# Linear attention with a maxout MLP on one core: the first k heads issued by ScalarE instead of SyncE

## The chip, the cores and the metric

The kernel runs on one core of one Trainium2 chip. The metric is device time in microseconds. The median of three runs before the change was 319.77 us (319.64 to 320.38).

## The reference

Inputs are q, k and v of shape (8 batches, 8 heads, 1024 positions, 64), two projections E and F of shape (64, 1024), and three MLP weights. All are float32.

```python
k_proj = np.einsum('ks,bhsd->bhkd', E, k)        # 1024 positions -> 64 rows
v_proj = np.einsum('ks,bhsd->bhkd', F, v)
attn   = softmax(q @ k_proj.T / sqrt(64))        # over the 64 rows
x      = (attn @ v_proj), heads side by side     # (8192, 512)
out    = np.maximum(x @ w1, x @ w2) @ w_out      # (8192, 512)
```

## The kernel before

TensorE does all the products in half precision. The batches of attention are worked one after the other, and the MLP of one batch is interleaved with the attention of the next through a list of slots that is written out by hand. Only the start of the program, batch 0, matters for the change.

The sequence on each engine is the order in which the program is written (a manual schedule). At the start:

- SyncE (queue q1 in the profile) issues three plain loads in float32: E into `ef_sb[:, 0]`, the first two heads of batch 0's k into `kf_sb`, and F into `ef_sb[:, 1]` (lines 86 to 88). `kf_sb` is "uncast": it arrives as float32 and is cast to half precision on the core.
- ScalarE loads its function table (line 89).
- GpSimd (queue q0) issues all the loads that cast to half precision on the way (line 108): heads 2 and 3 of k, heads 0 to 3 of q, heads 4 to 7 of k, heads 4 to 7 of q, then v in four pairs of heads. The MLP weights follow (lines 130, 139 and 143), each held back until earlier loads have landed.
- TensorE begins with eight filler matmuls on a tile of ones, `warm(8)` (line 153). Further `warm` calls stand between the steps of batch 0.

Then come the steps of batch 0 (lines 958 to 991), in this order on TensorE:

1. `step_eft(0)` transposes E (line 167); VectorE copies it out as `eft` (line 173).
2. The two heads in `kf_sb` are cast into `k_sb`: head 0 by VectorE (line 959), head 1 by ScalarE (line 960).
3. `step_kv(t, 0, 4, "k")` projects heads 0 to 3 of k (line 195). It needs `eft`, both casts, and GpSimd's heads 2 and 3.
4. `step_eft(1)` transposes F, `step_kpt` transposes the projected k (line 285), `step_qt` transposes q (line 311).
5. `step_sc` computes scores (line 340) and their exponentials on ScalarE (line 380); `step_dn` sums them (line 352) and takes the logarithm (line 388).
6. The same for heads 4 to 7, and then the projections of v (line 195 again), two heads at a time as v lands, followed by `step_at`, which applies the weights to v, and the first MLP products (line 524).

Of the kernel before, what the change touches and what calls it, by code (L numbers as in the profile page):

```python
# [19 lines left out]
def kernel(  # L20
# [12 lines left out]
    nc = tc.nc  # L33
# [5 lines left out]
    NC = S // 128  # L39
# [25 lines left out]
    def mm_bank(dtype=FP32, n=None):  # L65
        if n is None:
            n = turn.pop(0)
            turn.append(n)
        return ps.tile([128, 512 if dtype == FP32 else 1024], dtype, tag=f"mm{n}", name="mm_ps")
# [9 lines left out]
    def big(n, dtype=FP16):  # L79
# [3 lines left out]
    kf_sb = const.tile([128, 2048], FP32, tag="wo", name="kf_sb")[:, 0 : 2 * NC * D].rearrange(  # L83
        "p (h c d) -> p h c d", h=2, d=D
    )
    nc.sync.dma_start(out=ef_sb[:, 0, :], in_=E)
    nc.sync.dma_start(out=kf_sb, in_=k[0, 0:2].rearrange("h (p c) d -> p h c d", c=NC))
    nc.sync.dma_start(out=ef_sb[:, 1, :], in_=F)
    nc.scalar.add_instruction(
        mybir.InstLoadActFuncSet(  # L90
# [4 lines left out]
            outs=[],  # L95
        )
    )


    def alloc(t, n):  # L100
# [27 lines left out]
    for g in range(2):  # L128
        for w_sb, w in ((w2_sb, moe_w2), (w1_sb, moe_w1)):
            nc.gpsimd.dma_start(  # L130
                out=w_sb.rearrange("p (g z) f -> p g z f", z=2)[:, g, :, 0:256],
                in_=w.rearrange("(g p z) f -> p g z f", p=128, z=2)[:, g, :, 0:256],
            )
    for w_sb, w, f0, f1 in (
# [3 lines left out]
        for z in range(2):  # L138
            nc.gpsimd.dma_start(
                out=w_sb.rearrange("p (g z) f -> p g z f", z=2)[:, :, z, f0:f1],  # L140
                in_=w.rearrange("(g p z) f -> p g z f", p=128, z=2)[:, :, z, f0:f1],
# [994 lines left out]
    for i, (new, old) in enumerate(zip([*groups[1:], none], groups)):  # L1136
        n, h = divmod(i + 2, 2)
# [54 lines left out]
    for reg in regs:  # L1192
# [4 lines left out]
        out=mm_bank()[0:1, 0:1], lhsT=ones16[:, 0:1], rhs=ones16[:, 0:1], start=True, stop=True  # L1197
# [166 lines left out]
```

## Time and profile before

| | |
|---|---|
| median of 3 runs | 319.77 us |
| profiled execution, device time | 319.9 us |
| its span, first to last instruction | 318.1 us |
| TensorE busy | 312.3 us (98%) |
| VectorE, ScalarE, GpSimd busy | 241.1, 206.2, 40.8 us |
| GpSimd's DMA queue q0 | 30688 packets, 28.05 MB |
| SyncE's DMA queue q1 | 45664 packets, 24.85 MB |
| ScalarE's DMA queue q10 | 288 packets, 0.20 MB, all at the end of the run |

The profile is of one execution. Times in it count from the start of the program. A line of the timeline has the start, the duration, the engine, the line of the kernel, what is written and read, and in brackets the idle time of the engine just before and what ended it. SPq and ACTq are the DMA issues of SyncE and ScalarE. The profile does not give the landing time of loads issued by SyncE; it is read from the instruction that waited for them.

### The profile page before, as it was taken

To read this page: it belongs to the slowest core of one execution; us is meant where nothing else is said; L and a number is where in the kernel's file an instruction comes from. 1 tells how busy PE (TensorE), PEld (TensorE's weight loads), DVE (VectorE), ACT (ScalarE), POOL (GpSimd) and SP (SyncE) were. 2 spreads that over 40 slices of the span, in tenths; PEclk is the share of its full clock that TensorE was granted. 3 is DMA by queue.
4 is the path that set the end of the run, shared out by engine and by line. 5 is a ranking of instruction groups with operands and counts; after the bars stand their busy time and mean duration, and the time that the engine had idled before them with its cause. 6 is when DMAs were issued, how large, how long until landed. Compare 5 with 4: busy or idle time off the path is not lost.

```text
span 318.1 us, 9308 instructions
## 1 busy us (share of the span) xinstructions
PE 312.3 (98%) x3922; PEld 253.6 (80%) x3922; DVE 241.1 (76%) x441; ACT 206.2 (65%) x373; POOL 40.8 (13%) x63
## 2 busy tenths in 40 slices
PE   8989999999999999999999999999999999999996
PEld 3555588888887888788887888788887888888885
DVE  2366888877969696996969696996969696969883
ACT  2476842777776777477776778477776777765541
POOL 8259002003000300022000400030000000000000
PEclk9999999999999999999999999999999999999999
DMA  7999999999979999899999999989979131313124
GB/s 189 206 200 195 207 206 202 207 158 160 204 139 195 162 212 245 210 182 154 223 233 217 167 204 245 215 151 183 232 149 209 45 102 36 102 35 102 36 99 136
DMA packets 76684, 53.71 MB, mean 169 GB/s; under 512 B 29664, under 2 KB 76128, under 8 KB 76640
## 3 DMA queue, kind: packets, MB, share of 16 engines
q0 software_dynamic: 30688, 28.05, 56.0%
q1 hardware_dynamic: 45664, 24.85, 32.7%
q8 instruction: 31, 0.51, 0.6%
q10 hardware_dynamic: 288, 0.20, 0.2%
q14 instruction: 13, 0.11, 0.1%
HBM read 57.15 MB, written 16.78 MB: 232 GB/s over the span
## 4 chain that ended last, share of the span: by engine, by line
PE 92%; DMA 5%; POOL 1%; ACT 1%; issue 0%; DVE 0%; POOLq 0%
PE mm_ps L837 47%; PE mm_ps L745 27%; PE mm_ps L524 4%; DMA v_sb<-in_v_dram 4%; PE att_ps L352 3%; PE mm_ps L195 3%; PE mm_ps L340 2%; PE mm_ps L633 2%; PE att_ps L237 1%; DMA out_dram<-o_sb 1%; PE mm_ps L311 1%; POOL k_sb L108 0%; POOL q_sb L108 0%; ACT ld_sb L388 0%; ACT ex_sb L380 0%
## 5 line engine op out<-in xcount | busy, mean ns | idle before, releaser
L719 ACT COPY p_sb<-mm_ps 128x512 f32<-128x512 f32 x179 | 101.8, 592 | 49.1 <-PE mm_ps L745 27.2
L837 PEld LDWEIGHTS <-big 128*128 128x128 f16 x768 | 73.5, 98 | 11.8 <-issue 3.6
L837 PE MATMUL mm_ps<-T_sb,big 128*128 128x256 f16 x576 | 76.9, 273 | 0.0
L760 DVE TENSOR_TENSOR gt_sb<-mm_ps,p_sb 128x512 f16<-128x512 f32 x56 | 38.5, 687 | 43.0 <-PE mm_ps L745 41.6
L745 PE MATMUL mm_ps<-big,big 128*128 128x256 f16 x336 | 50.4, 273 | 0.0
L745 PEld LDWEIGHTS <-big 128*128 128x128 f16 x448 | 43.8, 98 | 5.1
L837 PE MATMUL mm_ps<-wo_sb,gt_sb 128*128 128x256 f16 x256 | 42.6, 273 | 0.0
L837 PEld LDWEIGHTS <-gt_sb 128*128 128x128 f16 x376 | 35.7, 98 | 6.7 <-issue 2.7
L469 ACT ACTIVATE ex_sb<-mm_ps 128x512 f16<-128x512 f32 x50 | 27.2, 596 | 18.0 <-PE mm_ps L340 12.3
L745 PEld LDWEIGHTS <-wd_sb 128*128 128x128 f16 x336 | 32.9, 98 | 3.8
L745 PE MATMUL mm_ps<-xt_sb,wd_sb 128*128 128x256 f16 x224 | 32.8, 273 | 0.0
L499 DVE TENSOR_TENSOR xt_sb<-att_ps,ld_sb 128x1024 f16<-128x1024 f32 x26 | 31.7, 1219 | 0.2
L837 PE MATMUL mm_ps<-m_sb,xt_sb 128*128 128x256 f16 x128 | 24.4, 273 | 0.0
L303 POOL COPY junk<-qt_sb 1x1 f16<-1x1 f16 x6 | 2.1, 346 | 172.5 <-DMA qt_sb<-q_sb 172.5
L868 DVE TENSOR_TENSOR o_sb<-mm_ps,p_sb 128x512 f32<-128x512 f32 x32 | 21.9, 683 | 2.8 <-ACT p_sb L897 2.0
L763 DVE TENSOR_SCALAR gt_sb<-gt_sb 128x512 f16<-128x512 f16 (+1 forms) x60 | 20.9, 348 | 2.1
L705 DVE TENSOR_TENSOR big<-gt_sb 128x1024 f16<-128x1024 f16 x32 | 21.8, 683 | 0.0
L837 PE MATMUL mm_ps<-wo_sb,big 128*128 128x256 f16 x128 | 21.5, 273 | 0.0
L806 ACT ACTIVATE gt_sb<-mm_ps 128x512 f16<-128x512 f32 x28 | 16.8, 601 | 5.7 <-PE mm_ps L745 5.7
L837 PE MATMUL mm_ps<-T_sb,gt_sb 128*128 128x256 f16 x120 | 20.3, 273 | 0.0
L837 PEld LDWEIGHTS <-xt_sb 128*128 128x128 f16 x188 | 18.3, 98 | 2.3 <-issue 0.2
L760 DVE TENSOR_TENSOR gt_sb<-p_sb 128x512 f16<-128x512 f32 x28 | 19.1, 682 | 0.6 <-ACT p_sb L719 0.6
(121 smaller groups left out, 434.7 us busy)
## 6 DMA issues: line engine op xcount, KB each, us to landing
out_dram<-o_sb SPq DMA_DIRECT2D x62, 256.0 KB
k_sb<-in_k_dram POOLq DMA_DIRECT2D x7, 1024.0 KB, 9.8
v_sb<-in_v_dram POOLq DMA_DIRECT2D x7, 1024.0 KB, 15.3
q_sb<-in_q_dram POOLq DMA_DIRECT2D x5, 1024.0 KB, 23.0
q_sb<-in_q_dram POOLq DMA_DIRECT2D x6, 512.0 KB, 15.8
big<-in_moe_w_dram POOLq DMA_DIRECT2D x12, 128.0 KB, 6.3
v_sb<-in_v_dram POOLq DMA_DIRECT2D x4, 256.0 KB, 13.6
wo_sb<-in_moe_w_out_dram POOLq DMA_DIRECT2D x1, 1024.0 KB, 10.4
```

The source lines that it names most:

```text
L195: nc.tensor.matmul(out=kv_ps[r * KP : (r + 1) * KP, h * D : (h + nh) * D], lhsT=eft[i][:, c, :], rhs=t[w][:, h0 + h : h0 + h + nh, c, :], ...
L469: nc.scalar.activation(out=t["ex", g, j][:, e, :], in_=banks[e], func=ACTF.Exp, scale=scale)
L499: nc.vector.tensor_tensor(out=x_out(t, g, j).rearrange("q z o n -> q o z n"), in0=at_ps.rearrange("q o (z n) -> q o z n", z=2), in1=ld[:, ...
L524: nc.tensor.matmul(out=h_ps, lhsT=wd_sb[:, r, fb * 128 : (fb + 1) * 128], rhs=t["xt"][:, r, :, j * W : (j + 1) * W], start=(r == 0), stop= ...
L705: nc.vector.tensor_tensor(out=S(i), in0=S(0) if x is None else x, in1=y(), op=op)
L719: copy(out=x, in_=bank)
L745: nc.tensor.matmul(out=bank[:, m * W : (m + 1) * W], lhsT=w_[:, n_, (2 * d + m) * 128 : (2 * d + m + 1) * 128], rhs=a[:, n_, :], start=(n ...
L760: nc.vector.tensor_tensor(out=c_blk(j, c), in0=two(x), in1=two(y), op=ALU.add)
L763: nc.vector.tensor_scalar_max(ap, ap, 0.0)
L806: nc.scalar.activation(out=out, in_=in_, func=ACTF.Relu)
L837: nc.tensor.matmul(out=bank[i][:, 0:CH] if two_banks else bank[:, i * CH : (i + 1) * CH], lhsT=a(c)[:, i * 128 : (i + 1) * 128], rhs=w_(c) ...
L868: nc.vector.tensor_tensor(out=o_sb, in0=two(x), in1=two(y), op=ALU.add)
```

## The change

SyncE no longer issues the load of `kf_sb`. ScalarE issues it, in its own DMA queue, as the instruction behind the table load. SyncE's queue holds E and then F. No other instruction is added, removed or moved.

```diff
     nc.sync.dma_start(out=ef_sb[:, 0, :], in_=E)
-    nc.sync.dma_start(out=kf_sb, in_=k[0, 0:2].rearrange("h (p c) d -> p h c d", c=NC))
     nc.sync.dma_start(out=ef_sb[:, 1, :], in_=F)
     nc.scalar.add_instruction(
         mybir.InstLoadActFuncSet(
...
     )
+    nc.scalar.dma_start(out=kf_sb, in_=k[0, 0:2].rearrange("h (p c) d -> p h c d", c=NC))
```

## The prediction

> **What bounds the kernel now.** I read the page first, then the chain of waits over the first 40 us, then the timeline of the first 20 us, then the DMA queues window by window. The page's chain says who sets the end:
>
> ```profile
> PE 92%; DMA 5%; POOL 1%; ACT 1%; issue 0%; DVE 0%; POOLq 0%
> ```
>
> TensorE carries 92% of it. The edited transfers matter only where TensorE is not yet the bound, in the start; a shift there moves everything behind it. The start of the chain, in order of time (start, us, what):
>
> ```profile
> 5.54 13.33 DMA v_sb<-in_v_dram
> 18.88 0.04 issue
> 18.92 0.64 PE mm_ps L195 x16
> ```
>
> So the start ends on a transfer of GpSimd's queue: the second quarter of v lands at 18.88, and its projection starts at 18.92. Before that the edited transfers count only if they delay TensorE past it. The timeline (start, duration, engine, line, in brackets the idle time before and its releaser):
>
> ```profile
> 1.26 0.83 POOL L108 DMA_DIRECT2D k_sb<-in_k_dram  x1 [0.80 <-POOLq L1348]
> 1.43 0.57 SPq L87 DMA_DIRECT2D kf_sb<-in_k_dram  x1
> ...
> 2.04 0.50 SPq L88 DMA_DIRECT2D big<-in_F_dram  x1
> ...
> 6.55 0.62 ACT L960 CAST k_sb<-kf_sb 128x512 f16<-128x512 f32 x1 [4.51 <-DMA kf_sb<-in_k_dram]
> 6.73 0.51 DVE L959 CAST k_sb<-kf_sb 128x512 f16<-128x512 f32 x1
> 7.29 0.79 PEld L195 LDWEIGHTS <-eft 128*64 128x64 f16 x8 [0.52 <-DVE k_sb L959]
> ```
>
> ScalarE waited 4.51 us for kf_sb, up to 6.55. Its cast ends at 7.17, VectorE's at 7.24, and the k projection starts at 7.29: a later landing of kf_sb delays TensorE at once, after a slack of about 0.07 us. Now what TensorE waits for near the end of the start:
>
> ```profile
> 17.34 0.41 PE L340 MATMUL att_ps<-qt_sb,kpt_sb 64*32 64x256 f16 x16
> 18.03 0.64 PE L195 MATMUL mm_ps<-v_sb,eft 128*64 128x128 f16 x16 [0.28 <-DMA v_sb<-in_v_dram]
> 18.92 0.64 PE L195 MATMUL mm_ps<-v_sb,eft 128*64 128x128 f16 x16 [0.25 <-DMA v_sb<-in_v_dram]
> ```
>
> Two waits for v, 0.28 + 0.25 = 0.53 us together, are the cushion that a delay from 7.29 meets before it reaches the end. The steps between offer none that I count: q lands just as the weight load at 10.35 wants it, and the rest runs back to back with the filler matmuls of L153, which stay the same in number.
>
> The queues (q1 is SyncE's, q0 GpSimd's; packets, MB, share of 16 engines), first from 3.25 to 4, then from 6.25 to 6.75, then from 7.25 to 8.25:
>
> ```profile
> q1 hardware_dynamic: 95, 0.19, 99.8%
> ```
> ```profile
> q1 hardware_dynamic: 46, 0.18, 96.5%
> q0 software_dynamic: 14, 0.01, 11.4%
> ```
> ```profile
> q0 software_dynamic: 194, 0.20, 123.1%
> ```
>
> kf_sb alone, in packets of 2 KB, goes at some 120 packets per us (90 without the 4-byte ones, in 0.75 us). GpSimd's packets (1 KB written, 2 KB read) reach 194 per us alone. F's 4 KB packets run from 6.06 to 7.0, behind the last of kf_sb; in that time GpSimd's queue nearly stands still.
>
> **The change, part by part.** The bytes stay the same: E and F 256 KB each, kf_sb 512 KB. In units of one 2 KB read these are 128, 128 and 256; GpSimd's first k transfer is 256 more.
>
> SyncE loses one issue of 0.57 us and gives F at 1.43 in place of 2.04. Nothing waits for SyncE then; its next issue is at 16.76. Worth nothing by itself.
>
> ScalarE gains one issue. No row has an issue behind a table load; two ACTq issues at the end of the run took 1.25 us, so 0.63 each. The table load runs from 0.75 to 2.03, so the issue is at 2.03 to 2.66. It lies in the 4.51 us in which ScalarE waits for this very transfer: cost nothing as an instruction; without that cover 0.63 us. Nothing is queued behind it on ScalarE but the cast that needs it.
>
> From issue to first packet: E was issued at 0.76 and its first packet ran at 2.16, so 1.40; the last ACTq store was issued at 314.20 and had no packet by 315.20, so over 1.0. kf_sb's first packet then comes at 3.0 to 3.4 (I take 3.4, the row that also opens a queue at the start). In the trace of before it came at 3.1, behind E. So the later issue costs only 0.3 us. What costs more is F, which now goes right behind E, ahead of or beside kf_sb.
>
> How late does kf_sb land? At 3.25 some 250 of its units are left, F's 128, and GpSimd's 256, which start at 4.1: 634. Up to 4.0 the engines carry 120 per us (one queue, the row above) or at most 200 (two at once, the 194): 90 to 150. From 4 to 5 the trace of before has 174 packets, the ceiling again 200. That leaves 284 to 370 at 5.0, and at 200 per us all three are through at 6.4 to 6.85. Before, kf_sb's last data ran at 6.05 and its cast began at 6.55. If kf_sb is the last of the three, the casts start 0.35 to 0.8 later, at 6.9 to 7.35; I take 7.15, a shift of 0.6. Less the slack of 0.07, TensorE's k projection starts 0.53 late, between 0.3 and 0.75.
>
> GpSimd's first k heads are needed by the same projection and share the same 6.4 to 6.85, so they bind no later than kf_sb with its cast of 0.62 us behind it.
>
> F is needed at 8.28, right behind the projection, and landed only just before, since its last data ran at 7.0. It now lands by about 6: worth at most 0.1 us, which I leave out.
>
> GpSimd's later transfers (q, k, q, v) decide the end. Either its stop around 6.5 was F's doing, and then it gains up to 0.43 us (97 packets in half a microsecond at 194, less the 14 that it moved), or its second transfer was not ready before 6.75, and it gains nothing. Its first 256 packets were just about used up by 6.25 (215 by 6.0, 45 in the quarter behind it), so I take the second: no gain, v at 18.88 as before.
>
> The sum: 0.53 late at the k projection, less 0.53 of waiting for v, is 0.0; with the ends 0.3 and 0.75 it is 0 to +0.2. For the parts of the cushion that I may overcount I add 0.1. The profiled execution took 319.9 us (318.1 of span, 1.8 around it), 0.13 above the median of 319.77. Forecast: 319.9 + 0.1 = **320.0 us**, practically no change.
>
> One rule of the Trainium skill speaks for little: DMA: Bandwidth & Descriptors, "Issuing engines are not separate DMA queues", says that transfers given by different engines run on the same 16 engines and interleave, so that spreading them saves only issue time. By it alone F's units would displace kf_sb's one for one, which is the lower rate in the sum above, and the sum would be +0.2. In this trace the single q1 ran below the later ceiling, which leaves room for two queues.
>
> **The rivals.**
>
> *Slower: kf_sb meets GpSimd's queue at full speed.* If ScalarE's issue waits for more than the table load's 1.28 us, kf_sb starts after 4.1 and shares packet for packet with q0. For a start at 4.6: 256 units at half of 200 per us are 2.6 us, so 7.2, and with the straggling of 0.75 that the last engine showed (29 units were left at 5.0, enough for 0.3 us, and it took until 6.05) 7.2 to 7.95; 0.5 more to the cast: 7.7 to 8.45. TensorE is 1.1 to 1.8 late, less the cushion 0.53: +0.6 to +1.3, about 321.1. It passes 0.3% when the cast starts after 8.1. The same price comes without a late issue if the slowest engine alone hands kf_sb on late: from 4.1 to 6.05 it moved some 8 packets, 0.25 us each, and six more would be 1.5 us. For it: the next ScalarE instruction in the trace is at 6.55, so nothing shows that it is free at 2.03. Against it: the rows show no activity of ScalarE after 2.03. The Trainium skill, ScalarE: Activation LUTs, "What ACT_TABLE_LOAD costs", adds a drain of about 1.38 us behind a load of 1.28; the load agrees with 1.28 here, the drain is not seen in any run, and with it the estimate is an issue at 3.4 and the upper part of this rival. A colder TensorE clock does not come into it: between 21 and 23 us TensorE is busy 0.72 and 0.53 of the time and the granted clock stays 1.00.
>
> *Faster: the queues run side by side.* If ScalarE gives the transfer while the table still loads (0.8), kf_sb runs beside E from 2.2, all three are through by about 5, and q0 has the engines to itself. q0 gains up to the 0.43 of the unused rate between 3.25 and 5 (634 - 284 against 634 - 370 units, 86 in all) and the 0.43 of the stop; TensorE loses nothing at 7.29, where the first cast holds it. The end comes earlier by 0.5 (the cushion, behind which TensorE itself is the bound) to 0.9: 319.0 to 319.4. Against it: q0's start at 4.1 and its second transfer may not depend on q1 at all.
>
> *It does not do what it says:* kf_sb was limited by its own 256 descriptors, not by its place, and lands as before: 319.9.
>
> **How the numbers follow.** About 0.3% (1 us) is what a measurement of this kernel can tell from no change. Forecast (0 to +0.4) 0.42; slower rival 0.34; faster rival 0.20, of which 0.11 past the bound, since it takes both its gains; no shift 0.04. Within 0.3%: 0.42 + 0.04 + 0.09 = 0.55; faster 0.11; slower 0.34. The range goes from 319.2 (-0.7, into the faster rival) to 321.3 (+1.4, the slower one's upper end).
>
> **What would show it.** An ACTq issue near 2.0 to 2.7 and F's 4 KB packets ahead of 4.5; ScalarE's first cast near 7.15 instead of 6.55; the k projection near 7.8; the waits of 0.28 and 0.25 for v mostly gone; the second v projection still at 18.9 to 19.1. A cast after 8.1 shows the slower rival, v landing before 18.5 the faster one. The forecast is wrong if the shift of the second v projection and that of the total differ by more than 0.3 us: then something behind the start moved.

## The result, and the profile after

The changed kernel takes 321.73 us in the median of 7 runs (320.11 to 323.0), against 320.04 (319.64 to 320.38) in now seven runs of the kernel before: 1.7 us longer, a ratio of 1.0051 with a 95% interval of 1.0037 to 1.0066. The prediction was 320.0 us, "practically no change", with 321.3 as its upper end; the result lies above that. The profiled execution took 322.0 us (span 320.2, before 318.1).

The page's chain now has no transfer of v, and less DMA:

```profile
PE 95%; DMA 2%; ACT 1%; DVE 1%; issue 0%
```

The chain of waits says what took the place of v in the start (start, us, what):

```profile
0.76 5.56 DMA big<-in_E_dram
6.32 0.14 issue
6.45 1.07 PE mm_ps L167 x8
7.52 1.79 PE mm_ps L153 x5
9.30 1.85 PE mm_ps L195 x8
```

The start hangs on E, which SyncE still issues first. The timeline of the changed kernel shows when everything is issued and used:

```profile
0.75 1.28 ACT L88 ACT_TABLE_LOAD   x1 [0.75 <-PEq L1348]
0.76 0.61 SPq L86 DMA_DIRECT2D big<-in_E_dram  x1
0.78 0.45 ACTq L97 DMA_DIRECT2D kf_sb<-in_k_dram  x1
...
1.42 0.57 SPq L87 DMA_DIRECT2D big<-in_F_dram  x1
...
5.02 0.62 ACT L960 CAST k_sb<-kf_sb 128x512 f16<-128x512 f32 x1 [2.98 <-DMA kf_sb<-in_k_dram]
...
6.45 1.07 PE L167 MATMUL mm_ps<-ident,big 64*128 64x64 f32 x8 [1.58 <-DMA big<-in_E_dram]
...
9.23 1.92 PE L195 MATMUL mm_ps<-k_sb,eft 128*64 128x256 f16 x8
```

Before the change, E's transposes and the k projection were these:

```profile
4.99 1.09 PE L167 MATMUL mm_ps<-ident,big 64*128 64x64 f32 x8
...
7.29 1.06 PE L195 MATMUL mm_ps<-k_sb,eft 128*64 128x256 f16 x8
```

ScalarE's issue does not stand behind the table load: it runs at 0.78, while the table loads. The k heads are cast from 5.02, which is 1.5 us earlier than before. But TensorE stands still for 1.58 us waiting for E, whose transposes begin at 6.45 in place of 4.99. And the k projection, 1.06 us long before, now takes 1.92.

The queues from 2 to 3.25 us and from 3.25 to 3.5 (q10 is ScalarE's, q1 SyncE's; packets, MB, share of the 16 DMA engines):

```profile
q10 hardware_dynamic: 183, 0.37, 88.5%
```
```profile
q10 hardware_dynamic: 48, 0.09, 91.7%
q1 hardware_dynamic: 5, 0.02, 24.0%
```

In the first of these windows q1 has no packet at all. E begins at 3.35, when the k heads are nearly through; before, it began at 2.16.

The trace records TensorE's granted clock in stretches of 3.41 us. The two that matter in the changed kernel (from:to, length, then the busy time and in brackets the instructions of TensorE, of its weight loads, of VectorE, ScalarE and GpSimd; then the granted clock, the DMA share and GB/s):

```profile
4.55:7.96 3.41, 1.83 (x13) 1.24 (x12) 0.41 (x1) 0.62 (x1) 3.15 (x5) 1.00 1.18 190
7.96:11.37 3.41, 3.41 (x15) 1.72 (x13) 0.80 (x3) 0.00 (x0) 0.70 (x1) 0.50 1.24 203
```

In the 3.41 us that contain the wait TensorE is busy for 1.83, and for the next 3.41 us its clock is halved. That is the 1.92 us of the k projection.

The steps of the profiled executions, as lateness in us against before. The last column is the first stretch of half clock after the clock had been full once, or the moment from which it was first full:

| | E transposes (4.99) | k projection (7.29) | F transposes (8.30) | first MLP product (23.32) | span (318.1) | TensorE clock |
|---|---|---|---|---|---|---|
| changed kernel | +1.46 | +1.94 | +2.78 | +2.05 | +2.1 | half 7.96 to 11.37 |
| the same, run again | +0.99 | +1.45 | +1.41 | +0.67 | +0.7 | full from 4.66 |

The two rows are the same kernel. Up to the k projection they differ by 0.5, and E's transposes already by as much. What holds the k projection itself is not the same: in the first row the five filler matmuls ahead of it run into the half clock (1.79 us in the chain above, 1.25 before) and end last; in the second it waits for heads 2 and 3, which GpSimd's queue brings:

```profile
8.74 1.03 PE L195 MATMUL mm_ps<-k_sb,eft 128*64 128x256 f16 x8 [0.52 <-DMA k_sb<-in_k_dram]
```

By the trace's completion records these heads landed at 7.12 before, and at 8.80 and 8.61 in the two rows: the new order made them late too, not only E. Between the k projection and the F transposes the first row then loses 0.84 to the half clock (the projection alone takes 1.92 - 1.06 = 0.86 longer). What reaches the end is the rest behind a cushion of 0.73 to 0.74.

### The profile page after: what moved, and what is told of

Read it like the earlier page. It is cut to its first block, busy times and chain, and to the rows that moved or that the text cites. A ratio compares the mean times of both kernels' runs of the same rounds, so it can differ in the third digit from the quotient of the medians.

```text
span 320.2 us, 9308 instructions
## 1 busy us (share of the span) xinstructions
PE 313.0 (98%) x3922; PEld 254.5 (79%) x3922; DVE 241.0 (75%) x441; ACT 206.2 (64%) x373; POOL 40.7 (13%) x63
## 4 chain that ended last, share of the span: by engine, by line
PE 95%; DMA 2%; ACT 1%; DVE 1%; issue 0%
PE mm_ps L837 46%; PE mm_ps L745 27%; PE mm_ps L524 4%; PE mm_ps L195 4%; PE att_ps L352 4%; PE mm_ps L340 2%; PE mm_ps L633 2%; DMA big<-in_E_dram 2%; PE mm_ps L153 1%; PE att_ps L237 1%; PE mm_ps L311 1%; PE mm_ps L167 1%; DMA out_dram<-o_sb 1%; ACT ex_sb L380 1%; PE att_ps L340 0%; DVE qt_sb L316 0%
```

## The experiments

After the result there were four theories. A: the k heads' packets go ahead of E's, E is late, and the idle TensorE loses its clock besides. B: two queues at once slow E, in whatever order. C: the clock costs nothing, since v holds the end anyway. D: E is slow for a reason other than GpSimd's queue beside it.

**The order alone, and the queue alone.** `e1_act_behind_e` leaves the k heads on ScalarE's queue, but behind E:

```diff
+    ones16 = const.tile([128, 512], FP16)
+    nc.vector.memset(ones16, 1.0)
+    nc.scalar.copy(out=flag, in_=ones16[0:1, 0:1])
     nc.scalar.dma_start(out=kf_sb, ...)
...
-    ones16 = const.tile([128, 512], FP16)
-    nc.vector.memset(ones16, 1.0)
```

> ScalarE still issues the two k heads in its own queue, but a one-element copy that waits for VectorE's tile of ones (ready at 1.41) stands before the issue, so that it comes at about 1.5, after E's issue (0.76 to 1.37). Theory A (the issue ran at 0.78 beside the table load, and the k heads' packets went ahead of E's): E is first again, its transposes start at 5.0 as before the change, the TensorE clock stays at 1.00, and the total is within 0.5 us of before (about 320). Rival B (two queues at once are what slows E, in whatever order): the E transposes stay late, 6 or more, and the total stays 1.5 to 2 us above before.

`e2_sp_kf_first` puts all three on SyncE's queue again, the k heads first:

```diff
+    nc.sync.dma_start(out=kf_sb, ...)
     nc.sync.dma_start(out=ef_sb[:, 0, :], in_=E)
-    nc.sync.dma_start(out=kf_sb, ...)
     nc.sync.dma_start(out=ef_sb[:, 1, :], in_=F)
```

> Everything on SyncE's queue as before the change, but in the order k heads, E, F. Theory A (what costs is E behind the k heads): E transposes near 6.4, a stretch of half clock, and a total 1.5 to 2 us above before, as with the change. Rival B (the second queue is the cause): E comes 512 KB later on one queue but without the contention, transposes before 5.8, clock 1.00, total within 0.6 us of before.

The first has 320.07 us, a ratio of 1.0005 (0.9996 to 1.0015) to before; the second 321.58, 1.0055 (1.0025 to 1.0085). Their timelines, e1 first:

```profile
0.76 0.61 SPq L86 DMA_DIRECT2D big<-in_E_dram  x1
...
1.42 0.57 SPq L87 DMA_DIRECT2D big<-in_F_dram  x1
1.45 0.45 ACTq L100 DMA_DIRECT2D kf_sb<-in_k_dram  x1
...
5.00 1.09 PE L168 MATMUL mm_ps<-ident,big 64*128 64x64 f32 x8
...
7.83 1.03 PE L196 MATMUL mm_ps<-k_sb,eft 128*64 128x256 f16 x8 [0.56 <-DMA k_sb<-in_k_dram]
```
```profile
0.75 0.46 SPq L86 DMA_DIRECT2D kf_sb<-in_k_dram  x1
...
1.27 0.59 SPq L87 DMA_DIRECT2D big<-in_E_dram  x1
...
7.65 1.06 PE L167 MATMUL mm_ps<-ident,big 64*128 64x64 f32 x8 [2.59 <-DMA big<-in_E_dram]
```

On ScalarE's queue with E ahead there is no loss; on one queue with E behind the k heads there is the whole loss (in the profiled execution, 323.1 us, E transposes +2.66, span +3.2, clock half from 9.08 to 12.50). Order is what costs, not the second queue: B falls. But e2 is not the changed kernel's loss in every part: E's transposes were expected near 6.4 and came at 7.65, since E took 3.92 us from its first packet to its last completion, against 2.36 before. Why is open, and the ten times of e2 reach from 319.83 to 323.9. In e1 the k projection is still 0.54 late, since it waits for GpSimd's heads; the first MLP product is 0.09 late.

`e10_ahead_of_table` is the changed kernel with ScalarE's issue written ahead of the table load (the two statements change places).

> The changed kernel with ScalarE's issue written ahead of the table load. If the table load never held the issue (it ran at 0.78 beside the load), the k heads' first packets are again near 1.9 to 2.0, E's at 3.35, and all is as with the change. If the load held it at all, the issue comes earlier by that.

The issue ran at 0.75 in place of 0.78, the k heads' first packets came in the same quarter of a microsecond, E's at 3.43; one time, 321.83 us. The table load held the issue by 0.03 us at most.

**One after the other, by the end of the issue.** `e5_act_e` gives E to ScalarE and leaves SyncE the k heads and F; `e6_act_behind_f` holds ScalarE's issue of the k heads until GpSimd's identity is there:

```diff
-    nc.scalar.dma_start(out=kf_sb, ...)
...
                 make_identity(nc, ident)
+                nc.scalar.copy(out=flag, in_=ident[0:1, 0:1])
+                nc.scalar.dma_start(out=kf_sb, ...)
```

> ScalarE issues E behind its table load; SyncE's queue carries the k heads and then F. Theory A in the form that the first runs left (one transfer after the other across both queues, in the order in which the issues end): whichever of the two issues ends first goes first. If that is E, its packets start near 1.9, its transposes at 5.0 (the fillers end there), clock 1.00, total within 0.4 us of before; if the k heads end first, E is late and the total is 1.5 us or more above. Rival B (two queues are served at once): E and the k heads have packets in the same quarters of a microsecond from 2 on, and both land late.

> The k heads on ScalarE's own queue, but issued only when GpSimd's identity is there (about 2.75), after both of SyncE's issues have ended (1.99). Theory A (one after the other, by the end of the issue, whichever the queue): the first packet of the k heads comes only when F's packets are through, near 5, as with all three on SyncE's queue in the order E, F, k heads (there 5.25), and the casts are near 8. Rival B (the two queues are served at once): the k heads have packets from about 3.9, beside F's, and the casts are near 7.

The timelines of e5, with E's transposes, and of e6, with a cast:

```profile
0.76 0.47 SPq L86 DMA_DIRECT2D kf_sb<-in_k_dram  x1
0.79 0.57 ACTq L97 DMA_DIRECT2D big<-in_E_dram  x1
...
6.48 1.07 PE L167 MATMUL mm_ps<-ident,big 64*128 64x64 f32 x8 [1.42 <-DMA big<-in_E_dram]
```
```profile
1.41 0.57 SPq L87 DMA_DIRECT2D big<-in_F_dram  x1
...
2.72 0.43 ACTq L122 DMA_DIRECT2D kf_sb<-in_k_dram  x1
...
9.99 0.62 ACT L961 CAST k_sb<-kf_sb 128x512 f16<-128x512 f32 x1 [7.09 <-DMA kf_sb<-in_k_dram]
```

In e5 the issue of the k heads ends at 1.23 and E's, on ScalarE, at 1.36; the k heads go first and E is late (transposes at 6.48, 321.63 us, ratio 1.0056, 1.0040 to 1.0073). In e6 the k heads have a queue of their own and are issued at 2.72, yet their first packet comes at 5.66, when F's are nearly through; casts at 9.99, one time of 324.85 us. That is the order that A expected, though later than its 5 and 8. All orders seen fit the same rule: in the changed kernel k (1.23) before E (1.37), in e1 k (1.90) before F (1.99), in e5 k before E. By the start of the issue it would be E first in the changed kernel (0.76 against 0.78) and F first in e1 (1.42 against 1.45). A preference for ScalarE's queue is excluded by e5. But in both pairs where start and end disagree it is the load of the k heads that ends first and goes first, so no run tells the end of the issue from some other advantage of that load, and no trace shows why it goes first.

**The order that the prediction had summed.** `e4_sp_kf_last` has E, F and then the k heads, all on SyncE's queue.

> SyncE's queue in the order E, F, k heads: the part of the change that the prediction priced, without ScalarE. By the prediction's sum the casts of the k heads start near 7.15 instead of 6.55, the k projection starts about 0.5 late, the clock stays at 1.00, and the total is 0 to 0.4 us above before. If the prediction's sum itself was wrong (the k heads meet GpSimd's queue and land after 8), the total is 0.6 to 1.3 us above before.

It took 321.76 us, 1.0062 (1.0032 to 1.0091).

```profile
8.34 0.62 ACT L960 CAST k_sb<-kf_sb 128x512 f16<-128x512 f32 x1 [6.31 <-DMA kf_sb<-in_k_dram]
```

Not 7.15 but 8.34: the k heads' packets began only at 5.31, behind the last of F. So the second alternative is right on the casts; the total, 1.7 us above before, is more than either has. The profiled execution (320.75 us) had the k projection 1.72 late and the first MLP product 0.94. The ten times split by the clock: the five with a mean granted clock of 0.995 or less take 322.1 to 324.2, the five above 320.1 to 321.4. In e2 they do not split so: its three slowest, 323.4 to 323.9, have a mean of 1.0.

**GpSimd's queue beside E.** `e7_gpsimd_held` lets GpSimd make its identity first and begin its loads only when E is there (`nc.gpsimd.tensor_copy(out=flag, in_=ef_sb[0:1, 0, 0:1])` ahead of them).

> The changed kernel, with all of GpSimd's loads held back until E has landed (a diagnosis, not a version to use: these loads come about 4 us later, so the total rises by 3 to 4 us). E's packets start at 3.35 behind the k heads as in the changed kernel. Theory A with GpSimd's queue as the reason that E then took 2.9 us for 64 packets in place of 1.1: E's packets are through by 4.6 and its transposes start by 5.6. Rival D (E is slow behind the k heads for another reason): transposes still at 6.2 or later.

E's transposes began at 6.03, between the two forecasts. With GpSimd's loads beside E, other executions of the changed start have 5.90 (e9), 5.96 (e10), 5.98 (run again) and 6.45, so holding GpSimd's queue back shows no gain. The trace's records of packets and completions say the same. From E's first packet to its last completion it took 2.36 us before (2.16 to 4.52) and 2.54 in e7; with the changed start it took 2.38 to 2.47 in e3, e8, e9, e10 and the second profile of the changed kernel, and 2.96 in its first. So in most executions E's transfer is hardly slower behind the k heads; it begins 1.2 to 1.4 us later. What stretched it in the first profile, in e5 (2.76) and in e2 is open. The time, 323.01 us, holds the later loads.

**The clock.** Three runs tried to keep TensorE busy while it waits for E: 15 fillers in place of 8 (`e3_more_fillers`), eight longer ones (`e8_long_fillers`), and the five fillers behind the transposes moved in front (`e9_fillers_moved`, 13 and 0 in place of 8 and 5).

> The changed kernel with 15 filler matmuls in place of 8 ahead of the E transposes, so that TensorE stays busy until about 6.4 while it waits for E. Theory A with the clock as a part of its cost: the transposes stay at about 6.45, the granted clock stays at 1.00, the k projection and what follows lose the 0.9 us of the half clock, total about 0.8 to 1.0 us below the changed kernel. Rival C (the clock costs nothing, since the v landings hold the end anyway): total as the changed kernel, within 0.3 us.

> The changed kernel with the same number of instructions, its eight fillers made longer (the tile of ones read as float32, 256 columns) so that TensorE is busy until about 6.4. The run with 15 fillers kept the clock and gained 0.5 us up to the last matmul, but its end came 2.7 us later behind that matmul, which I put down to its added instructions. Theory A with the clock as a part: clock 1.00 throughout, first MLP products 0.5 to 0.9 us earlier than in the changed kernel, total 0.5 to 0.9 us below it, no longer end. Rival C (the clock is worth nothing): total within 0.3 us of the changed kernel.

> The changed kernel with the five fillers behind the E transposes moved in front of them (13 and 0 in place of 8 and 5), so that the number of instructions stays and TensorE is busy until about 5.95 while it waits for E. Theory A with the clock as a part: transposes still at 6.4, clock 1.00 in the first 20 us, the k projection takes 1.1 in place of 1.9 us, first MLP products 0.5 to 0.9 us earlier than in the changed kernel and the total as much lower, near 321.0; the end behind the last matmul as before. Rival C (the clock is worth nothing): total within 0.3 us of the changed kernel run beside it.

`e3` took 323.85 us (1.0110, 1.0073 to 1.0147), `e8` 324.44 (1.0141, 1.0115 to 1.0167), `e9` 323.05 (1.0087, 1.0065 to 1.0109). All miss the total that was expected, for two reasons.

In e3 the clock stayed at 1.00 from 4.22 on, and the first MLP product came 1.20 late in place of 2.05: a gain of 0.85, in the range expected for the clock. At the k projection it was still as late as the changed kernel (1.98 against 1.94), so the gain lies behind it, where the half clock had been. But its last matmul, at 317.68, is followed by 4.6 us before the end of the span, where before it is 1.9. e8 has the same tail; its fillers were also too long (the transposes began at 7.81), so it tells nothing on the clock. Both programs have more instructions (9322 and 9324 in place of 9308; e8 was meant to have the same number), and none of those with 9308 to 9310 has the tail. Its cause was not tested.

In e9 the move only shifted the idle time behind the transposes, where TensorE waits for GpSimd's heads and had no fillers left:

```profile
4.18:7.59 3.41, 2.65 (x16) 1.45 (x13) 0.58 (x1) 0.62 (x1) 3.41 (x5) 1.00 0.97 184
7.59:11.00 3.41, 2.15 (x24) 1.91 (x24) 0.86 (x3) 0.05 (x1) 0.80 (x2) 1.00 1.18 189
11.00:14.42 3.42, 3.42 (x28) 2.34 (x25) 1.09 (x3) 0.53 (x1) 0.85 (x2) 0.50 1.24 203
```

The clock holds behind the stretch with 2.65 us of work and is halved behind the one with 2.15. The profiled k projection was 1.56 late, yet the first MLP product 2.11: here the clock cost more than the cushion gave back. All ten executions show 0.995 or less.

**The changed kernel once more**, beside e9:

> The changed kernel itself, beside the run with moved fillers. Theory A: E's transposes 1 to 2 us late again and a median 1.2 to 2 us above before; the single times spread over 2 to 3 us, where before spreads over 1, because the stretch of half clock comes in some executions and not in others.

321.25 us (320.56 to 323.79), ratio 1.0044 (1.0017 to 1.0072). Its profiled execution kept the clock:

```profile
4.66:8.07 3.41, 2.36 (x14) 1.36 (x13) 0.99 (x2) 0.58 (x1) 3.03 (x5) 1.00 0.99 175
8.07:11.48 3.41, 2.90 (x28) 2.22 (x28) 0.74 (x3) 0.58 (x1) 0.78 (x2) 1.00 1.23 204
```

With 2.36 us of work in the stretch, the next one stays at 1.00, and the total is 320.56. So C falls: between the k projection and the F transposes the two profiled executions of one kernel differ by 0.88, and e3 agrees. D is left only for the executions in which E's transfer was stretched, as above. No run beat the kernel before; e1 equals it.

The spread of the ten times is as expected, but the clock is not shown to make all of it: only one of the ten has a mean clock below 0.999 (322.02 us), and the slowest, 323.79, has 1.0. The mean can hide lost clock at the start. In e10 the profile records the clock only from 10.79 on, as full, and gives a mean of 1.0, yet the k projection there took 1.80 us and the F transposes were 2.68 late. Nor is the kernel before quite free of it: one of its 19 executions in this series took 322.98 us, with a mean of 0.989.

## Why the prediction was wrong

1. **"So the issue is at 2.03 to 2.66."** It was at 0.78 to 1.23. The prediction took the program's order for the order in time. It did name this case, as the condition of its *faster* rival, and gave it 0.20.

2. **"kf_sb runs beside E from 2.2"** (the faster rival's mechanism) and **"room for two queues"** (the forecast's upper rate). The transfers ran one after the other. The trace of before shows one queue at work so: F's first packet came at 6.06, when the last of the k heads ran at 6.05, though F's issue had ended at 2.54. No row of its start shows what two such queues do beside each other, so both readings were guesses. The Trainium skill, DMA: Bandwidth & Descriptors, "Issuing engines are not separate DMA queues", says that transfers of different engines interleave, and that pointed the same wrong way. Here the two hardware queues did not interleave (q1 with no packet from 2 to 3.25, and an overlap only between 3.25 and 4.5, where the last packets of the k heads ran), and the measurement decides.

3. **What is late next, when E is late, was never asked.** E's transposes began where the first fillers end, at 4.99, so the trace of before showed no wait for E; by its last completion at 4.52, its slack was 0.34 us (0.47, less the 0.13 that also passes between landing and transposes in the changed kernel). E's lateness is a term that the prediction put at nothing without a reason. In the first profile its first packet came 1.19 later (3.35 - 2.16) and its transfer took 0.60 longer; less the slack, that is the 1.46 at the transposes. In the second it was 1.28 and 0.04, and 0.99 at the transposes.

4. **"they bind no later than kf_sb"**, of GpSimd's first k heads. They landed 1.5 to 1.7 us later than before, and with the clock kept they were the last thing that the k projection waited for (0.52 us). In e1, with E on time, they alone made it 0.54 late. By the completion records their landing goes with the order: 8.37 and 9.20 in e5 and e2, where the k heads also go first, 7.70 in e1, 6.64 in e4, where they go last.

5. **"A colder TensorE clock does not come into it."** It cost 0.84 us behind the k projection of the first profile, besides the longer fillers ahead of it. The row that was quoted, 0.72 and 0.53 busy from 21 to 23, covers 2 us; what counted was the work in a stretch of 3.41 us. The two stretches that hold that row have 2.85 and 3.23 us of work, the one that opened in the start had 1.83.

6. **The sum for the k heads (casts at 7.15)** was wrong on its own ground too: in the order that it assumed, e4 measured 8.34. It shared the engines out among three transfers, where F went entirely first.

7. **The slower rival** had the right sign and came nearer to the measured 1.7 (+0.6 to +1.3, chance 0.34), but by luck: in its mechanism the k heads land late, and they came early, with E late in their place.

What held: the cushion ahead of the second v projection, though 0.53 was too small (0.73 to 0.74 from the F transposes to the first MLP product, in the changed kernel's two executions and in e4 and e5); that ScalarE's issue costs nothing as an instruction; and that what is left behind the start shifts the end one for one (+2.05 at the first MLP product, +2.1 at the end).

The sum with the measured terms, for the profiled execution: E's transposes 1.46 late, 0.48 more at the k projection (GpSimd's heads land later, and the fillers ahead of it run into the half clock and end last), 0.84 for the half clock behind it, less 0.73 of cushion: +2.05. With the clock kept: 0.99 + 0.46 (GpSimd's heads) - 0.04 - 0.74 = +0.67. So the late loads alone cost a size that the prediction had allowed for, by another way; the half clock made the rest.

## What to carry to other kernels

Moving a transfer to another engine's queue can also move it in the order in which the transfers are served. Write down when each issue starts and *ends*, on all queues, and ask who is behind the transfer that moved up. Before costing the transfer that is moved, cost those that it overtakes, above all where the trace shows no wait for them, since their slack may be small. A wait that opens on TensorE in the start can cost twice: as idle time, and as the work that is missing in that stretch of the clock.

## What the runs showed of the hardware

- A DMA issue on ScalarE's queue runs during a table load (0.78, inside 0.75 to 2.03); written ahead of it, in e10, it came 0.03 earlier. In e1 ScalarE's first instruction behind the load ran at 2.05, right at the load's end at 2.03, so the drain of 1.38 us that the slower rival reckoned with was not there.
- Loads that SyncE and ScalarE issue were served one after the other, in the order in which the issues ended, in all orders tried (changed kernel, e1, e5, e6). Whether the end of the issue is what decides is not shown. Loads of GpSimd's queue did run beside them (from 4 to 5 us in the changed kernel 62 packets of q1 and 42 of q0).
- TensorE's clock was granted by stretches of 3.41 us: halved after 0.72 (e6), 1.43 (e2), 1.71 (e7), 1.83 and 2.15 (e9) us of work in one, kept after 2.26 (e7), 2.36 and 2.40 (e4). The half clock lasted one stretch, in e6 two. The stretches lie at another place in each execution, so that the same kernel had the half clock in one profile and not in the next. The Trainium skill, TensorE: Matmul & The Clock Gate, "Why this matters for your kernels", asks for no gaps above about 3 us; here a gap of 1.58 us was enough. The Trainium skill, TensorE: Matmul & The Clock Gate, Part 1, says that the window of 3413 ns runs free, and this agrees with the stretches' length and places.
